# Batch 0's k over SyncE's queue with one add on VectorE, softmax in double steps, batch 1's attention placed late in tile 0

## The chip, the cores and the metric

One core of one Trainium2 chip. The metric is the device time of one execution in microseconds (us), lower is better. The profile's span (first to last instruction) is some 2 us shorter than that time. A run's state is "fast" or "slow"; only fast runs are compared. In the profiles PE is TensorE (PEld its weight loads), DVE is VectorE, ACT ScalarE, POOL GpSimd and SP SyncE.

## The reference

```python
# q, k, v: batch 8, heads 8, sequence 576, head size 64, float32
k_p = k.reshape(B, H, 72, 8, D).mean(axis=3)       # pooled over 8 rows
v_p = v.reshape(B, H, 72, 8, D).mean(axis=3)
scores = q @ k_p.T / sqrt(D)                       # softmax over 72
x = (softmax(scores) @ v_p)                        # to 4608 tokens x 512
h = x @ w_in                                       # 512 -> 2048
out = (h * cos(h)) @ w_out                         # 2048 -> 512
```

## The kernel before

The program order of each engine is as written. Tokens are worked in nine tiles of 512: an up-projection (64 matmuls of 512 columns), then a down-projection (64 more). A batch has 576 tokens, so tile t needs batches up to t (tile 8 up to 7); batch t+1's attention, for the next tile, is woven between the down matmuls of tile t. Batch 0's attention comes first, alone. The kernel uses PSUM as six banks in three pairs (`banks`) and two single ones (`obanks`). Cut and abridged:

```python
def step(b, i, pair):                    # one of 8 softmax steps of a batch: head pair i//2, half i%2
    cs, ao = pair[:, 0, :], pair[:, 1, :]
    sums(b, i, cs)                       # 2 matmuls with ones
    values(b, i, ao)                     # 2 matmuls with pooled v
    inverse(b, i, cs)                    # ScalarE: Ln, then Exp(-x)
    normal(b, i, ao)                     # VectorE: xT = ao * inverse
...
load_kv_cast(0, "k", k, 2)               # all of these on GpSimd's queue, fp32 cast to bf16
...
load_q(0, 2)
load_kv_cast(0, "v", v)
for cg in range(4): load_w_in(cg)
load_kv_cast(1, "k", k); load_q(1); load_kv_cast(1, "v", v)
for cg in range(4): load_w_out(cg)
...
    if t == 0:                           # batch 1: transposes and pooling ahead of the down-projection
        ...
        fill = [(i * 7 // 2, f) for i, f in enumerate(main)]
    else:                                # later batches
        early = [k_transpose, q_transpose, q_transpose_rem]        # written as lambdas
        main = att_main(b, [banks[1], banks[0]], banks[2])         # two score pairs, one pair for steps
        fill = [(4 + 4 * i, f) for i, f in enumerate(early)]
        fill += [(16 + (i * 5) // 2, f) for i, f in enumerate(main)]   # entry, before which down matmul
```

The softmax here doesn't subtract the row's maximum and nothing guards it: scores larger than these inputs give would overflow.

## Time and profile before

| | before |
|---|---|
| time, median of 4 runs | 361.46 us (360.49 to 362.04) |
| span of the profiled run | 358.6 us |
| batch 0's attention | 0 to 30.6 us |
| tile 0, up and down | 30.6 to 78.1 us |
| each of six tiles with attention | 36.80 us |
| each of two tiles without | 27.6 us |

The stages are read from the chain of waits, where the up-projections stand out as rows of 40 to 64 matmuls. "Starts effectively" below is the time at which an up-projection without a gap would have had to start to be where it is.

### The profile page before, as it was taken

What the parts mean: (1) busy time and instruction counts of PE and PEld (TensorE: products, weight loads), DVE (VectorE), ACT (ScalarE), POOL (GpSimd) and SP (SyncE); (2) the same over time, 40 slices, a digit from 0 to 9 for tenths busy, and PEclk for the clock granted to TensorE, in tenths of its full rate; (3) what the DMA queues carried; (4) which work ended last, traced back from release to release, by engine and by line L of the source; (5) the groups of instructions that cost most, each with busy time, mean ns of one, the idle gap of its engine ahead of it and who ended that gap; (6) DMA issues with size and microseconds to landing.
All of it is one profiled execution on the core that took longest, in us unless ns stands there. A gap on an engine that the chain in (4) does not pass through costs nothing.

```text
span 358.6 us, 4924 instructions
## 1 busy us (share of the span) xinstructions
PE 328.5 (92%) x1958; PEld 137.6 (38%) x1992; DVE 156.4 (44%) x201; ACT 191.8 (53%) x280; POOL 126.9 (35%) x84
## 2 busy tenths in 40 slices
PE   2787979989998999899989998999899999999995
PEld 2332532334423443344234432443244324444442
DVE  0222741136623672357235733573347434723731
ACT  1472634646575657655675666565656575602610
POOL 8533219800990089108910693059200000000000
PEclk9999987999999999999999999999999999999999
DMA  8999995179426951686087707680110001012011
GB/s 99 190 205 200 223 184 96 14 170 181 84 60 95 197 98 56 99 177 118 29 124 162 133 31 125 139 155 29 50 41 0 31 36 54 0 59 60 0 54 63
DMA packets 31494, 35.18 MB, mean 98 GB/s; under 512 B 5936, under 2 KB 20528, under 8 KB 31472
## 3 DMA queue, kind: packets, MB, share of 16 engines
q0 software_dynamic: 20224, 13.64, 27.0%
q1 hardware_dynamic: 11248, 21.24, 25.1%
q8 instruction: 15, 0.25, 0.3%
q14 instruction: 7, 0.06, 0.0%
HBM read 36.70 MB, written 9.44 MB: 129 GB/s over the span
## 4 chain that ended last, share of the span: by engine, by line
PE 88%; DVE 3%; ACT 3%; issue 2%; DMA 2%; POOL 1%; DVEq 0%; POOLq 0%
PE bank L258 35%; PE obank L266 34%; PE bank L199 4%; PE bank L208 4%; PE bank L222 3%; PE bank L168 2%; PE bank L150 2%; PE bank L266 2%; DVE xT L227 2%; DMA q_main<-in_q_dram 2%; ACT inv L214 1%; ACT lnc L212 1%; POOL k_b L87 1%; DVE o_sb L271 1%; DVE qT L171 1%
## 5 line engine op out<-in xcount | busy, mean ns | idle before, releaser
L266 PE MATMUL obank<-w_out_sb,g_sb 128*128 128x512 bf16 x522 | 138.0, 383 | 2.6 <-issue 2.1
L258 PE MATMUL bank<-xT,w_in_sb 128*128 128x512 bf16 x566 | 126.7, 382 | 0.8 <-issue 0.3
L262 ACT ACTIVATE cos<-bank,half_pi 128x1024 f32<-128x1024 f32 x72 | 80.2, 1114 | 75.7 <-PE bank L258 75.1
L263 DVE TENSOR_TENSOR g_sb<-bank,cos 128x1024 bf16<-128x1024 f32 x72 | 88.2, 1225 | 54.0 <-ACT cos L262 54.0
L117 POOL TENSOR_TENSOR kv_st<-kv_st 72x2048 f32<-72x2048 f32 x12 | 54.2, 4518 | 105.8 <-DMA kv_st<-in_k_dram 105.8
L258 PEld LDWEIGHTS <-w_in_sb 128*128 128x128 bf16 x576 | 56.5, 98 | 69.1 <-issue 2.4
L266 PEld LDWEIGHTS <-g_sb 128*128 128x128 bf16 x576 | 45.9, 98 | 60.0 <-issue 15.0
L227 DVE TENSOR_TENSOR xT<-bank,inv 128x288 bf16<-128x288 f32 x64 | 29.3, 458 | 88.9 <-ACT inv L214 84.7
L202 ACT ACTIVATE ex<-bank 72x576 bf16<-72x576 f32 x64 | 41.0, 641 | 36.7 <-PE bank L199 35.2
L212 ACT ACTIVATE lnc<-bank 128x288 f32<-128x288 f32 x56 | 23.0, 411 | 32.2 <-PE bank L222 32.2
L271 DVE COPY o_sb<-obank 128x512 f32<-128x512 f32 x34 | 23.4, 687 | 29.4 <-PE obank L266 29.4
L214 ACT ACTIVATE inv<-lnc 128x288 f32<-128x288 f32 x64 | 28.3, 443 | 2.0
L118 POOL TENSOR_TENSOR kv_st<-kv_st 72x1024 f32<-72x1024 f32 x12 | 28.2, 2349 | 0.9
L208 PE MATMUL bank<-ex,ones 72*64 72x288 bf16 x112 | 17.5, 307 | 6.3 <-DVE xT L227 6.3
L222 PE MATMUL bank<-ex,vp 72*64 72x288 bf16 x128 | 20.1, 303 | 3.1 <-DVE xT L227 3.1
L199 PE MATMUL bank<-qT,kpT 64*72 64x288 bf16 x128 | 21.5, 331 | 0.5 <-DVE qT L183 0.5
L208 PEld LDWEIGHTS <-ones 72*64 72x64 bf16 x128 | 8.5, 109 | 32.7 <-issue 32.7
L199 PEld LDWEIGHTS <-kpT 64*72 64x72 bf16 x128 | 7.4, 110 | 27.0 <-issue 27.0
L171 DVE COPY qT<-bank 128x2048 bf16<-128x2048 bf16 (+1 forms) x9 | 9.9, 1106 | 4.2 <-PE bank L168 4.2
L168 PE MATMUL bank<-identity,q_main 128*64 128x128 bf16 x256 | 9.7, 232 | 2.0 <-DMA q_main<-in_q_dram 1.2
L246 ACT ACT_TABLE_LOAD x8 | 10.3, 1283 | 0.9 <-PEq L389 0.7
L249 ACT ACT_TABLE_LOAD x8 | 10.3, 1283 | 0.1
(36 smaller groups left out, 109.0 us busy)
## 6 DMA issues: line engine op xcount, KB each, us to landing
out_dram<-o_sb SPq DMA_DIRECT2D x32, 256.0 KB, 2.3
kv_st<-in_k_dram SPq DMA_DIRECT2D x5, 1024.0 KB, 8.6
kv_st<-in_v_dram SPq DMA_DIRECT2D x5, 1024.0 KB
q_main<-in_q_dram POOLq DMA_DIRECT2D x7, 512.0 KB, 6.1
w_in_sb<-in_moe_w_in_dram POOLq DMA_DIRECT2D x4, 512.0 KB, 12.1
w_out_sb<-in_moe_w_out_dram POOLq DMA_DIRECT2D x4, 512.0 KB, 13.7
v_b<-in_v_dram POOLq DMA_DIRECT2D x2, 512.0 KB, 12.0
kv_st<-in_k_dram POOLq DMA_DIRECT2D x1, 1024.0 KB, 18.7
```

Source lines behind the costliest of these rows:

```text
L117: eng.tensor_tensor(out=s[:, :, 0:4, :], in0=s[:, :, 0:4, :], in1=s[:, :, 4:8, :], op=ADD)
L118: eng.tensor_tensor(out=s[:, :, 0:2, :], in0=s[:, :, 0:2, :], in1=s[:, :, 2:4, :], op=ADD)
L199: nc.tensor.matmul(pair[:Sp, hp, :SEG], lhsT=kpT[hp * 64:hp * 64 + 64, pj, :], rhs=qT[hp * 64:hp * 64 + 64, pj, sg * SEG:(sg + 1) * SEG])
L202: nc.scalar.activation(out=ex, in_=pair[:Sp, :, :SEG], func=ACTF.Exp, scale=scale / POOL)
L208: nc.tensor.matmul(cs[hp * 64:hp * 64 + 64, :SEG], lhsT=ones[:Sp, :], rhs=ex[:, hp, :])
L214: nc.scalar.activation(out=inv, in_=lnc, func=ACTF.Exp, scale=-1.0)
L222: nc.tensor.matmul(ao[hp * 64:hp * 64 + 64, :SEG], lhsT=vp[:, 2 * pj + hp, :], rhs=ex[:, hp, :])
L227: nc.vector.tensor_mul(out=xT[:, pj, c0:c0 + SEG], in0=ao[:, :SEG], in1=att.pop(("inv", b, i)))
L258: nc.tensor.matmul(h[:, j, :], lhsT=w_in_sb[fc // 4][:, ki, (fc % 4) * 128:(fc % 4 + 1) * 128], rhs=xT[:, ki, t * TILE:(t + 1) * TILE], st ...
L262: nc.scalar.activation(out=cos, in_=h, func=ACTF.Sin, bias=half_pi[:, :1])
L263: nc.vector.tensor_mul(out=g_sb[:, 2 * fp:2 * fp + 2, :], in0=h, in1=cos)
L266: nc.tensor.matmul(o, lhsT=g_sb[:, fc, ms * 128:(ms + 1) * 128], rhs=w_out_sb[fc // 4][:, fc % 4, :], start=(fc == 0), stop=(fc == FFCH - 1))
```

## The change

Its intent: get the first q earlier by moving k off GpSimd's queue; have fewer, longer softmax instructions; and let tile 0's down-projection run before batch 1's data are needed, with the output weights loaded earlier for it. The core of the diff, abridged (lambdas and other lines are left out):

```diff
+    def load_k_halves(b):                       # fp32, no cast, SyncE's queue
+        for j in range(2):
+            st = kvst.tile([Sp, H, POOL, D], FP32, ...)[:, 0:hs]
+            ... nc.sync.dma_start(out=o, in_=i.rearrange("h p n -> p h n"))
+    def pool_k_half(b, j, bank):
+        nc.vector.tensor_tensor(out=kb, in0=st[:, :, 0:4, :], in1=st[:, :, 4:8, :], op=ADD)
+        pool_k_mm(b, bank, kb, range(2 * j, 2 * j + 2))      # 4 rows left instead of 8
...
+    def sums(b, j, sg, cs):                     # two head pairs: 4 matmuls, Ln and Exp of 2 x 288
+    def values(b, j, sg, ao):                   # 4 matmuls; normal() multiplies 2 x 288 at once
+    def att_main(b):
+        sc, cs, ao = banks[0], banks[1], banks[2]            # one score pair
...
-    load_kv_cast(0, "k", k, 2)
+    load_k_halves(0)
+    load_q(0, 2)
...
+    for cg in range(4):
+        load_w_out(cg)                          # ahead of batch 1's k, q, v
...
+            if t == 0:
+                early = [pool_k_mm(1), q_transpose(1), q_transpose_rem(1), pool_v_mm(1)]
+                at, first, gap = [36, 44, 46, 50], 48, 1
+            else:
+                at, first, gap = [2, 6, 10], 14, 3
+            fill = list(zip(at, early))
+            fill += [(first + gap * i, f) for i, f in enumerate(att_main(b))]
```

Batch 0's order on PE also changes: the first scores come before the second half of k and q, and v is pooled before all values.

More of the change, by code (lines that the diff above doesn't have):

```diff
@@ L40 @@
     SEG = S // 2
-    NSTEP = 2 * KCH
     EX = 6
@@ L48 @@
     wpool = ctx.enter_context(tc.tile_pool(name="wpool", bufs=1))
-    kvb = ctx.enter_context(tc.tile_pool(name="kvb", bufs=4))
+    kvb = ctx.enter_context(tc.tile_pool(name="kvb", bufs=3))
     kvst = ctx.enter_context(tc.tile_pool(name="kvst", bufs=2))
@@ L79, in load_kv, with load_kv_cast @@
         staged[which, b] = st
-    def load_kv_cast(b, which, src, halves=1):
+    def load_kv_cast(b, which, src):
         st = kvb.tile([Sp, H, POOL, D], BF16, name=f"{which}_b", tag="kv_b")
-        hs = H // halves
-        for j in range(halves):
-            for o, i in by_rows(st[:, j * hs:(j + 1) * hs].rearrange("p h t d -> p h (t d)"),
-                                kv_view(src, b)[j * hs:(j + 1) * hs]):
-                nc.gpsimd.dma_start(out=o, in_=i.rearrange("h p n -> p h n"))
-        staged[which, b] = st
+        for o, i in by_rows(st.rearrange("p h t d -> p h (t d)"), kv_view(src, b)):
+            nc.gpsimd.dma_start(out=o, in_=i.rearrange("h p n -> p h n"))
+        staged[which, b] = st
+    def load_k_halves(b):
+        hs = H // 2
+        for j in range(2):
+            st = kvst.tile([Sp, H, POOL, D], FP32, name="kv_st", tag="kv_st")[:, 0:hs]
+            for o, i in by_rows(st.rearrange("p h t d -> p h (t d)"), kv_view(k, b)[j * hs:(j + 1) * hs]):
+                nc.sync.dma_start(out=o, in_=i.rearrange("h p n -> p h n"))
+            staged["k", b, j] = st
     def load_q(b, halves=1):
@@ L131, in heads, with pool_k_mm @@
         return x[:, 2 * pj:2 * pj + 2]
-    def pool_k_mm(b, bank, pjs):
-        kb = staged["k", b]
+    def pool_k_mm(b, bank, kb, pjs):
         if ("kpT", b) not in att:
             att["kpT", b] = asb.tile([128, KCH, Sp], BF16, name="kpT", tag="kpT")
-        ps = bank[:, 0:KCH * Sp].rearrange("p (j n) -> p j n", j=KCH)
-        for pj in pjs:
-            for t in range(POOL):
+        n, rows = len(pjs), kb.shape[2]
+        ps = bank[:, 0:n * Sp].rearrange("p (j n) -> p j n", j=n)
+        for i in range(n):
+            for t in range(rows):
                 for hp in range(2):
-                    nc.tensor.matmul(ps[hp * 64:hp * 64 + 64, pj, :], lhsT=kb[:, 2 * pj + hp, t, :],
-                                     rhs=identity[:Sp, :Sp], start=(t == 0), stop=(t == POOL - 1))
-        sl = slice(pjs[0], pjs[-1] + 1)
-        nc.vector.tensor_copy(out=att["kpT", b][:, sl, :], in_=ps[:, sl, :])
+                    nc.tensor.matmul(ps[hp * 64:hp * 64 + 64, i, :], lhsT=kb[:, 2 * i + hp, t, :],
+                                     rhs=identity[:Sp, :Sp], start=(t == 0), stop=(t == rows - 1))
+        nc.vector.tensor_copy(out=att["kpT", b][:, pjs[0]:pjs[-1] + 1, :], in_=ps)
+    def pool_k_half(b, j, bank):
+        st = staged.pop(("k", b, j))
+        kb = asb.tile([Sp, H // 2, POOL // 2, D], BF16, name="k_sum", tag="k_sum")
+        nc.vector.tensor_tensor(out=kb, in0=st[:, :, 0:4, :], in1=st[:, :, 4:8, :], op=ADD)
+        pool_k_mm(b, bank, kb, range(2 * j, 2 * j + 2))
     def pool_v_mm(b, bank):
@@ L162, in q_transpose @@
         n = len(pjs)
-        ps = bank.rearrange("p a n -> p (a n)").bitcast(BF16)[:, 0:n * 512].rearrange(
+        if len(bank.shape) == 3:
+            bank = bank.rearrange("p a n -> p (a n)")
+        ps = bank.bitcast(BF16)[:, 0:n * 512].rearrange(
             "p (j t n) -> p j t n", t=4, j=n)
@@ L193, in k_transpose, with scores @@
         att["kpT", b] = kpT
-    def scores(b, i, pair):
-        pj, sg = i // 2, i % 2
+    def scores(b, pj, sg, pair):
         kpT, qT = att["kpT", b], att["qT", b]
@@ L202, in scores @@
         nc.scalar.activation(out=ex, in_=pair[:Sp, :, :SEG], func=ACTF.Exp, scale=scale / POOL)
-        att["ex", b, i] = ex
-    def sums(b, i, cs):
-        ex = att["ex", b, i]
-        for hp in range(2):
-            nc.tensor.matmul(cs[hp * 64:hp * 64 + 64, :SEG], lhsT=ones[:Sp, :], rhs=ex[:, hp, :])
-    def inverse(b, i, cs):
-        lnc = asb.tile([128, SEG], FP32, name="lnc", tag="lnc")
-        nc.scalar.activation(out=lnc, in_=cs[:, :SEG], func=ACTF.Ln)
-        inv = asb.tile([128, SEG], FP32, name="inv", tag="inv", bufs=EX)
+        att["ex", b, pj, sg] = ex
@@ L214, in inverse @@
+    def sums(b, j, sg, cs):
+        for i in range(2):
+            ex = att["ex", b, 2 * j + i, sg]
+            for hp in range(2):
+                nc.tensor.matmul(cs[hp * 64:hp * 64 + 64, i, :SEG], lhsT=ones[:Sp, :], rhs=ex[:, hp, :])
+        lnc = asb.tile([128, 2, SEG], FP32, name="lnc", tag="lnc", bufs=1)
+        nc.scalar.activation(out=lnc, in_=cs[:, :, :SEG], func=ACTF.Ln)
+        inv = asb.tile([128, 2, SEG], FP32, name="inv", tag="inv")
         nc.scalar.activation(out=inv, in_=lnc, func=ACTF.Exp, scale=-1.0)
-        att["inv", b, i] = inv
@@ L217, in values @@
-    def values(b, i, ao):
-        ex = att.pop(("ex", b, i))
+        att["inv", b, j, sg] = inv
+    def values(b, j, sg, ao):
         vp = pooled["v", b]
-        pj = i // 2
-        for hp in range(2):
-            nc.tensor.matmul(ao[hp * 64:hp * 64 + 64, :SEG], lhsT=vp[:, 2 * pj + hp, :], rhs=ex[:, hp, :])
-    def normal(b, i, ao):
-        pj, sg = i // 2, i % 2
-        c0 = b * S + sg * SEG
-        nc.vector.tensor_mul(out=xT[:, pj, c0:c0 + SEG], in0=ao[:, :SEG], in1=att.pop(("inv", b, i)))
@@ L229, in step @@
-    def step(b, i, pair):
-        cs, ao = pair[:, 0, :], pair[:, 1, :]
-        sums(b, i, cs)
-        values(b, i, ao)
-        inverse(b, i, cs)
-        normal(b, i, ao)
-    def att_main(b, score_pairs, value_pair):
-        n = len(score_pairs)
-        main = [lambda: scores(b, 0, score_pairs[0])]
-        for i in range(NSTEP):
-            if i + 1 < NSTEP:
-                main.append(lambda i=i: scores(b, i + 1, score_pairs[(i + 1) % n]))
-            main.append(lambda i=i: step(b, i, value_pair))
+        for i in range(2):
+            pj = 2 * j + i
+            ex = att.pop(("ex", b, pj, sg))
+            for hp in range(2):
+                nc.tensor.matmul(ao[i][hp * 64:hp * 64 + 64, :SEG], lhsT=vp[:, 2 * pj + hp, :], rhs=ex[:, hp, :])
@@ new lines, in normal, with score, value, f @@
+    def normal(b, j, sg, ao):
+        c0 = b * S + sg * SEG
+        inv = att.pop(("inv", b, j, sg))
+        if isinstance(ao, list):
+            for i in range(2):
+                nc.vector.tensor_mul(out=xT[:, 2 * j + i, c0:c0 + SEG], in0=ao[i][:, :SEG], in1=inv[:, i, :])
+        else:
+            nc.vector.tensor_mul(out=xT[:, 2 * j:2 * j + 2, c0:c0 + SEG], in0=ao[:, :, :SEG], in1=inv)
+    def att_main(b):
+        todo = [(j, sg) for sg in range(2) for j in range(2)]
+        sc, cs, ao = banks[0], banks[1], banks[2]
+        def score(n, i):
+            j, sg = todo[n]
+            return lambda: scores(b, 2 * j + i, sg, sc)
+        def value(n):
+            j, sg = todo[n]
+            def f():
+                values(b, j, sg, [ao[:, 0, :], ao[:, 1, :]])
+                normal(b, j, sg, ao)
+            return f
+        main = [score(0, 0), score(0, 1)]
+        for n, (j, sg) in enumerate(todo):
+            if n + 1 < len(todo):
+                main.append(score(n + 1, 0))
+            main.append(lambda j=j, sg=sg: sums(b, j, sg, cs))
+            if n + 1 < len(todo):
+                main.append(score(n + 1, 1))
+            main.append(value(n))
@@ L289 @@
     nc.gpsimd.memset(half_pi, math.pi / 2.0)
-    load_q(0, 2)
     load_kv_cast(0, "v", v)
@@ L297 @@
     load_kv_cast(1, "v", v)
-    for cg in range(4):
-        load_w_out(cg)
     load_kv(2, "k", k, nc.gpsimd)
@@ L303 @@
     exp_tables()
-    LAG = 4
-    for j in range(2):
-        pjs = range(2 * j, 2 * j + 2)
-        pool_k_mm(0, obanks[j], pjs)
-    for j in range(2):
-        pjs = range(2 * j, 2 * j + 2)
-        q_transpose(0, banks[2 * j], pjs)
-        q_transpose_rem(0, banks[1][:, 0, :], pjs)
-    for i in range(2):
-        scores(0, i, banks[i])
-    for i in range(NSTEP + LAG):
-        if i < NSTEP:
-            sums(0, i, obanks[i % 2])
-            inverse(0, i, obanks[i % 2])
-            if i + 2 < NSTEP:
-                scores(0, i + 2, banks[i % 2])
-        if i == LAG - 1:
-            pool_v_mm(0, banks[2][:, 0, :])
-        if i >= LAG:
-            values(0, i - LAG, banks[2][:, 0, :])
-            normal(0, i - LAG, banks[2][:, 0, :])
+    pool_k_half(0, 0, obanks[0])
+    q_transpose(0, banks[2], range(0, 2))
+    q_transpose_rem(0, banks[2][:, 1, :], range(0, 2))
+    scores(0, 0, 0, banks[0])
+    scores(0, 1, 0, banks[1])
+    pool_k_half(0, 1, obanks[1])
+    q_transpose(0, obanks[0], range(2, 4))
+    q_transpose_rem(0, obanks[1], range(2, 4))
+    sums(0, 0, 0, banks[2])
+    scores(0, 0, 1, banks[0])
+    scores(0, 1, 1, banks[1])
+    pool_v_mm(0, obanks[1])
+    todo = [(0, 0), (0, 1), (1, 0), (1, 1)]
+    for n, (j, sg) in enumerate(todo):
+        values(0, j, sg, obanks)
+        normal(0, j, sg, obanks)
+        if n + 1 < 4:
+            sums(0, *todo[n + 1], banks[2])
+        if n + 2 < 4:
+            for i in range(2):
+                scores(0, 2 * todo[n + 2][0] + i, todo[n + 2][1], banks[i])
     sin_tables()
@@ L330 @@
             up(t, fp)
-            if t == 0 and fp == 5:
-                pool_k_mm(1, obanks[0], range(KCH))
         more = b < B
+        mms = [(ms, fc) for ms in range(4) for fc in range(FFCH)]
         fill = []
-        if t == 0:
-            outs = [obanks[0], obanks[1], banks[2][:, 0, :], banks[2][:, 1, :]]
-            mms = [(ms, fc) for cg in range(4) for ms in range(4) for fc in range(4 * cg, 4 * cg + 4)]
-            exp_tables()
-            q_transpose(1, banks[0])
-            q_transpose_rem(1, banks[1][:, 0, :])
-            pool_v_mm(1, banks[1][:, 1, :])
-            main = att_main(1, [banks[0]], banks[1])
-            fill = [(i * 7 // 2, f) for i, f in enumerate(main)]
-        else:
-            outs = [obanks[ms % 2] for ms in range(4)]
-            mms = [(ms, fc) for ms in range(4) for fc in range(FFCH)]
-            if more:
+        if more:
+            if t == 0:
+                early = [lambda: pool_k_mm(b, banks[0][:, 0, :], staged["k", b], range(KCH)),
+                         lambda: q_transpose(b, banks[1]),
+                         lambda: q_transpose_rem(b, banks[0][:, 1, :]),
+                         lambda: pool_v_mm(b, banks[2][:, 0, :])]
+                at, first, gap = [36, 44, 46, 50], 48, 1
+            else:
                 early = [lambda: k_transpose(b, banks[2][:, 0, :]),
@@ L350 @@
                          lambda: q_transpose_rem(b, banks[2][:, 1, :])]
-                main = att_main(b, [banks[1], banks[0]], banks[2])
-                fill = [(4 + 4 * i, f) for i, f in enumerate(early)]
-                fill += [(16 + (i * 5) // 2, f) for i, f in enumerate(main)]
-                exp_tables()
-        if more and t > 0 and b + 1 < B:
-            load_kv(b + 1, "k", k)
-            load_kv(b + 1, "v", v)
-            load_q(b + 1)
+                at, first, gap = [2, 6, 10], 14, 3
+            fill = list(zip(at, early))
+            fill += [(first + gap * i, f) for i, f in enumerate(att_main(b))]
+            fill.sort(key=lambda x: x[0])
+            exp_tables()
+            if t > 0 and b + 1 < B:
+                load_kv(b + 1, "k", k)
+                load_kv(b + 1, "v", v)
+                load_q(b + 1)
         fi = 0
@@ L363 @@
                 fi += 1
-            down_mm(outs[ms], ms, fc)
+            down_mm(obanks[ms % 2], ms, fc)
             if fc == FFCH - 1:
-                down_out(t, ms, outs[ms])
+                down_out(t, ms, obanks[ms % 2])
         while fi < len(fill):
```

## The prediction

> **What bounds the kernel now.** I first read the page's chain that ended last, by engine, then cut the span into stages: batch 0's attention, token tile 0 (up-projection, then down-projection with batch 1's attention between its matmuls), six equal tiles that each carry one more batch's attention, and two tiles without attention.
>
> The chain by engine:
>
> ```profile
> PE 88%; DVE 3%; ACT 3%; issue 2%; DMA 2%; POOL 1%; DVEq 0%; POOLq 0%
> ```
>
> Stretches of the span (start:end, length; busy time of PE, PEld, DVE, ACT, POOL with instructions in brackets; granted clock, DMA's busy share, GB/s):
>
> ```profile
> 0.00:31.00 31.00, 18.01 (x157) 9.01 (x159) 6.39 (x15) 13.18 (x26) 17.48 (x32) 1.00 1.16 169
> 31.00:49.80 18.80, 17.46 (x158) 8.59 (x159) 10.34 (x11) 10.11 (x9) 4.20 (x6) 1.00 1.24 206
> 49.80:78.28 28.48, 25.36 (x122) 8.95 (x125) 7.51 (x15) 13.37 (x26) 17.79 (x8) 0.88 0.63 98
> 78.28:115.08 36.80, 35.45 (x214) 14.38 (x216) 17.72 (x23) 22.88 (x34) 17.79 (x8) 1.00 0.60 116
> ...
> 299.08:326.70 27.62, 27.51 (x127) 12.54 (x128) 12.56 (x12) 8.91 (x8) 0.00 (x0) 1.00 0.10 39
> ```
>
> The tile without attention takes 27.62 us for 128 matmuls of 512 columns: 0.216 us each, PE without a gap. No change to waits can shorten that. A tile with attention takes 36.80, so its attention costs 9.2 us of PE's time; there are six. The share of DMA, over 1, says that it is saturated through the first two stretches and TensorE's clock granted at 0.88 in the third. The gains can lie in attention's 9.2 us per tile and in the first 78 us.
>
> PE's own waits (total, times, longest):
>
> ```profile
> PE obank L142 <- DMA k_b<-in_k_dram: 6.9, 2, 5.5
> PE bank L208 <- DVE xT L227: 6.3, 7, 0.9
> PE bank L222 <- DVE xT L227: 3.1, 6, 0.6
> ...
> PE bank L150 <- DVE qT L183: 1.1, 1, 1.1
> ```
>
> The second line is the steady loss: once per tile, 0.9 us. The timeline of a steady tile shows where: the last softmax step follows the one before it after only two down matmuls, and both use one PSUM pair, so PE waits for the normalisation:
>
> ```profile
> 111.65 0.46 DVE L227 TENSOR_TENSOR xT<-bank,inv 128x288 bf16<-128x288 f32 x1 [0.85 <-ACT inv L214]
> ...
> 112.16 0.31 PE L208 MATMUL bank<-ex,ones 72*64 72x288 bf16 x2 [0.93 <-DVE xT L227]
> ```
>
> The third line of waits is batch 0's tail, where one bank serves all values: the seven last normalisations follow each other at 1.07 us. Its timeline also shows:
>
> ```profile
> 10.13 1.07 PE L168 MATMUL bank<-identity,q_main 128*64 128x128 bf16 x16 [0.90 <-DMA q_main<-in_q_dram]
> ...
> 13.32 0.65 ACT L202 ACTIVATE ex<-bank 72x576 bf16<-72x576 f32 x1 [11.30 <-PE bank L199]
> ...
> 18.30 3.63 PE L150 MATMUL bank<-v_b,identity 72*72 72x512 bf16 x8
> ```
>
> **What the Trainium skill says.** "TensorE: Matmul & The Clock Gate", part 1: 512 columns take 426.7 ns while the array is cold, 215.7 ns once it has been busy some 3.4 us. The trace agrees: 0.216 above, but weight loads 0.425 apart in v's pooling (18.7 to 20.9) and in the first up matmuls (31.4 to 33.9). "ScalarE: Activation LUTs", What ACT_TABLE_LOAD costs: 186 ns plus 0.833 ns per element with immediate operands. 288 elements give 426 (trace: 411 for Ln, 443 for the inverse), 576 give 666 (trace: 641 for the softmax Exp). So doubling an activation saves one fixed part. "VectorE: DVE Perf Modes": two-source fp32 runs at one element per cycle of 0.96 GHz; 1024 of them are 1067 ns before overhead; the trace's 1024-element product, one source in PSUM, takes 1225. "DMA: Bandwidth & Descriptors", Issuing engines are not separate DMA queues: another issuing engine saves only issue time. The trace shows what that is on GpSimd: 0.57 to 0.79 us per issue, with four k issues ahead of q's first.
>
> **The change, part by part.**
>
> *Batch 0.* k goes as fp32 over SyncE, so q is issued from about 1.2 us instead of 4.4. Both share the bandwidth, so I put k's first half at about 5, q's at 7 (q was used at 10.1), second halves by 9. Added: per k half a VectorE add of 72x1024, about 1.1 us; removed: half of the pooling matmuls (32 took 1.17, 16 take 0.6). Scores now precede the second half: q transposes 7.0 to 8.1, copies to 9.0, first Exp about 9.4 instead of 13.3. But that isn't the gain, because v stands in PE's order before the values: v was issued at 7.1 and landed 7.6 later, near 15. The same 3.5 MB of fp32 come ahead of its end, started half a microsecond earlier, so I take 14.2. Pooling cold 3.6, copy 0.7: values begin at about 18.9. The chain from there, by the durations above (Ln 0.65, inverse 0.68, Exp 0.64, cold matmul groups 0.4 to 0.5): second sums 0.45 later, Ln, inverse and two Exps end at +3.55, third sums, Ln, inverse, two Exps at +6.8, fourth sums, Ln, inverse at +8.7, two products of 0.46 at +9.7. The first up group needs the last of these for its fourth chunk, so the up-projection effectively starts at +8.5 = 27.4. Before: 30.6. **Gain 3.2.**
>
> *Tile 0.* Up from 27.4: 64 x 0.216 = 13.8, plus 1.7 for eight cold ones; batch 1's k pooling (1.2) has left it: ends 42.9 (before 47.4). Down: 36 matmuls 7.8, k pooling 1.3, 8 matmuls 1.7, q transposes 1.2, and 1.7 until both copies to qT are done (they end after PE has passed the remainder and four matmuls, so 0.4 of it is idle): first score at 56.6. From there entries come after every single down matmul, and ScalarE is nearly the bound: 8 Exps of 0.64, 4 Ln and 4 inverses make 10.4 us, while the one score pair lets PE run only one Exp ahead. Walking the 16 entries in order, with 1.9 for v's warm pooling, I get PE waits of about 0.5 at four scores and the last sums, and 0.85 in the next up-projection for the last product: 14.8 us. Tile 1 starts at 71.4, before 78.1: **gain 6.7 in all, 3.5 beyond batch 0.** What pays is what the third stretch lost: PE idle 0.73, 0.64 and 1.1 around batch 1's q and v, and the cold clock after it.
>
> *Output weights first.* They land about 8 us earlier, k, q and v of batch 1 some 8 us later (v at about 43 instead of 35). Both are ahead of use (42.9 for weights, 52 for k, past 56 for v). Worth nothing by itself; it is what the later placing of batch 1 permits.
>
> *Six steady tiles.* PE's work is unchanged: one score group and one step cost together 1.905 (start to start of scores) less five down matmuls 1.08 = 0.83; eight make 6.6, k and q transposes 1.6, the wait 0.93, together 9.1 of the 9.2. After: still 8 score pairs, 8 sum pairs, 8 value pairs in 16 entries, now 3 matmuls apart, the last two too. The last sums have their Exp ready about 0.6 early and the last values find their bank free; 0.93 goes. New: scores use one pair only. A score reaches its Exp in 0.35 and frees the bank 0.64 later, 1.0 in all; the next score comes 0.24 + 3 x 0.216 + 0.1 = 1.0 later, so the first three scores of a tile may wait 0.05 to 0.1. Net 0.83 x 6 = **5.0**. Fewer, longer VectorE and ScalarE instructions save busy time that PE doesn't wait for. The last two tiles don't change.
>
> Sum: 6.7 + 5.0 = 11.7; 361.6 - 11.7 = about 350.
>
> **Rivals.**
> - *The single score pair becomes the bound in steady tiles.* The 1.0 against 1.0 above speaks for it at the tile's start; against it, later scores are two entries apart (2 us). A wait of 0.8 per tile would undo the 5.0: 355.
> - *Tile 0's packed softmax runs by ScalarE's latency, or the array goes cold again.* 16 entries within 16 matmuls; if each of 8 scores waits 0.5 more, +4; half clock over 5 us costs 2.5. Against: PE still has some 80% to do in that stretch. 353 to 354.
> - *v lands no earlier, or later, because k's queue takes turns with GpSimd's.* Each microsecond goes straight to the end: 351 to 352. If it lands at 13, PE isn't at the pooling before about 13.5 and the gain is up to 0.7 more: 349.
> - *All of batch 0's head start reaches the end* (first Exp 4 us earlier): 349. Against: v, above.
>
> **Range and chances.** The steady part is safest (0.93 seen in every tile), tile 0 the least safe, and it errs both ways by 3 us. Two per cent is 354.4, which needs two rivals at once. Predicted 350, range 346 to 354.
>
> **What would show it.** Steady tiles of about 35.95 without a wait for xT at the sums; short waits at the first scores for Exp. First Exp near 9.4; v's pooling at 14 to 15, in cold steps of 0.425; first up matmul near 27.5; tile 1 from about 71.4, clock 1.00 in tile 0's down-projection. Wrong if steady tiles stay at 36.5 or more, or tile 1 starts after 75.

## The result and the profile after

| | before | after |
|---|---|---|
| time, median of 4 runs | 361.46 us | 351.08 us (350.99 to 351.85) |
| ratio | | 0.972 (95% interval 0.9695 to 0.9746) |
| span | 358.6 us | 349.2 us |

A ratio is the mean time of one kernel's fast runs over that of the other's in the same rounds, so it is not quite the ratio of the medians. All outputs are right.

In the chain that ended last, PE's share is as it was:

```profile
PE 88%; ACT 4%; DMA 4%; DVE 1%; POOL 1%; issue 1%; ACTq 0%; POOLq 0%
```

The stretches of the kernel after (columns as in the prediction): batch 0, tile 0's up-projection, its down-projection with batch 1, two steady tiles, a tile without attention.

```profile
0.00:31.10 31.10, 15.53 (x126) 7.40 (x127) 7.95 (x15) 10.71 (x17) 14.48 (x27) 1.00 1.26 175
31.10:46.40 15.30, 14.74 (x63) 6.29 (x62) 8.54 (x9) 9.37 (x9) 4.76 (x8) 1.00 1.39 197
46.40:74.65 28.25, 25.89 (x223) 11.64 (x222) 9.43 (x13) 13.11 (x19) 17.82 (x8) 1.00 0.71 130
74.65:110.54 35.89, 35.62 (x215) 14.27 (x215) 17.19 (x20) 21.91 (x27) 17.77 (x8) 1.00 0.75 128
110.54:146.43 35.89, 35.89 (x218) 14.39 (x216) 17.07 (x19) 21.64 (x27) 17.80 (x8) 1.00 0.60 113
303.79:331.42 27.63, 27.63 (x130) 12.54 (x128) 12.57 (x13) 8.90 (x8) 0.00 (x0) 1.00 0.12 39
```

The steady tile is 0.91 shorter and PE has no gap in it: in the fifth row its busy time is the stretch. The first row ends half a microsecond later than batch 0's stage did before. Its clock of 1.00 is no measurement: the trace's clock records begin with the first change (at 34.2 here, 33.8 before), and the view counts the time before as full clock. PE's own waits in the whole kernel after (total, times, longest):

```profile
PE obank L146 <- DVE k_sum L153: 11.4, 2, 8.5
PE bank L221 <- ACT ex L214: 1.8, 3, 0.8
PE bank L211 <- ACT ex L214: 1.3, 3, 0.5
PE bank L284 <- DVE xT L243: 0.9, 1, 0.9
...
PE obank L159 <- DMA v_b<-in_v_dram: 0.8, 1, 0.8
```

The sums (L221) no longer wait for xT anywhere. Of the three waits of sums for Exp two are in batch 0; the three of scores (L211) and the one of the up-projection (L284) are tile 0's. None is in a steady tile. Batch 0's timeline:

```profile
7.22 1.22 DVE L153 TENSOR_TENSOR k_sum<-kv_st 72x1024 bf16<-72x1024 f32 x1 [7.22 <-DMA kv_st<-in_k_dram]
...
11.38 1.18 ACT L214 ACTIVATE ex<-bank 72x576 bf16<-72x576 f32 x2 [9.36 <-PE bank L211]
...
13.24 1.22 DVE L153 TENSOR_TENSOR k_sum<-kv_st 72x1024 bf16<-72x1024 f32 x1 [1.89 <-DMA kv_st<-in_k_dram]
...
14.52 0.69 PE L146 MATMUL obank<-identity,k_sum 72*64 72x72 bf16 x16 [2.94 <-DVE k_sum L153]
...
18.31 3.60 PE L159 MATMUL obank<-v_b,identity 72*72 72x512 bf16 x8 [0.79 <-DMA v_b<-in_v_dram]
```

The first Exp came 1.9 earlier than before (13.3), but then PE waited 2.94 for k's second half, which landed only at 13.2. That put it at v's pooling at 17.5, and there it waited 0.79 more for v, which landed at 18.2 (near 15.3 before). So the head start was lost at k's second half, and the last 0.8 of it at v.

| stage | before, us | after, us | gain | predicted |
|---|---|---|---|---|
| up-projection of tile 0 starts effectively | 30.6 | 31.1 | -0.5 | 3.2 |
| tile 1 starts effectively | 78.28 | 74.65 | 4.1 more | 3.5 more |
| six steady tiles | 6 x 36.80 | 6 x 35.89 | 5.5 | 5.0 |
| sum | | | 9.1 | 11.7 |

Both times of tile 1 are boundaries of the stretches; the 78.1 above and in the prediction is the record of the first matmul itself, 0.16 earlier. The span fell by 9.4; the small rest is in the tail and in the boundaries read to a tenth. By medians the time fell by 10.4.

### The profile page after: what moved, and what is told of

The parts are those of the page before. It is cut to its first block, busy times and chain, and to the rows that moved or that the text cites. A ratio compares the mean times of both kernels' runs of the same rounds, so it can differ in the third digit from the quotient of the medians.

```text
span 349.2 us, 4752 instructions
## 1 busy us (share of the span) xinstructions
PE 326.5 (93%) x1960; PEld 136.4 (39%) x1960; DVE 154.3 (44%) x175; ACT 181.6 (52%) x216; POOL 124.4 (36%) x80
## 4 chain that ended last, share of the span: by engine, by line
PE 88%; ACT 4%; DMA 4%; DVE 1%; POOL 1%; issue 1%; ACTq 0%; POOLq 0%
PE obank L292 38%; PE bank L284 36%; PE bank L211 4%; DMA v_b<-in_v_dram 4%; PE bank L221 3%; PE bank L234 3%; PE bank L179 2%; ACT inv L225 1%; ACT lnc L223 1%; ACT ex L214 1%; PE obank L159 1%; PE bank L159 0%; POOL q_main L100 0%; PE bank L191 0%; DVE qT L182 0%
## 5 line engine op out<-in xcount | busy, mean ns | idle before, releaser
L292 PE MATMUL obank<-w_out_sb,g_sb 128*128 128x512 bf16 x576 | 148.6, 381 | 0.0
L284 PE MATMUL bank<-xT,w_in_sb 128*128 128x512 bf16 x576 | 127.6, 382 | 1.4 <-DVE xT L243 0.9
L284 PEld LDWEIGHTS <-w_in_sb 128*128 128x128 bf16 x576 | 56.6, 98 | 71.0 <-issue 4.3
L243 DVE TENSOR_TENSOR xT<-bank,inv 128x576 bf16<-128x576 f32 x28 | 21.2, 758 | 67.7 <-PE bank L234 49.3
L297 DVE COPY o_sb<-obank 128x512 f32<-128x512 f32 x36 | 24.9, 691 | 41.5 <-PE obank L292 41.0
L223 ACT ACTIVATE lnc<-bank 128x576 f32<-128x576 f32 x32 | 20.8, 650 | 28.2 <-PE bank L221 27.9
L225 ACT ACTIVATE inv<-lnc 128x576 f32<-128x576 f32 x32 | 21.9, 683 | 1.0
L211 PE MATMUL bank<-qT,kpT 64*72 64x288 bf16 x128 | 20.4, 323 | 1.5 <-ACT ex L214 1.3
L211 PEld LDWEIGHTS <-kpT 64*72 64x72 bf16 x128 | 8.0, 111 | 25.1 <-issue 25.1
L221 PE MATMUL bank<-ex,ones 72*64 72x288 bf16 x128 | 15.6, 315 | 2.0 <-ACT ex L214 1.8
L234 PE MATMUL bank<-ex,vp 72*64 72x288 bf16 x112 | 12.2, 298 | 0.0
L146 PE MATMUL obank<-identity,k_sum 72*64 72x72 bf16 x32 | 1.4, 256 | 11.4 <-DVE k_sum L153 11.4
L221 PEld LDWEIGHTS <-ones 72*64 72x64 bf16 x128 | 5.5, 113 | 14.8 <-issue 14.5
```

The lines of the kernel that those rows point to most:

```text
L211: nc.tensor.matmul(pair[:Sp, hp, :SEG], lhsT=kpT[hp * 64:hp * 64 + 64, pj, :], rhs=qT[hp * 64:hp * 64 + 64, pj, sg * SEG:(sg + 1) * SEG])
L221: nc.tensor.matmul(cs[hp * 64:hp * 64 + 64, i, :SEG], lhsT=ones[:Sp, :], rhs=ex[:, hp, :])
L223: nc.scalar.activation(out=lnc, in_=cs[:, :, :SEG], func=ACTF.Ln)
L225: nc.scalar.activation(out=inv, in_=lnc, func=ACTF.Exp, scale=-1.0)
L284: nc.tensor.matmul(h[:, j, :], lhsT=w_in_sb[fc // 4][:, ki, (fc % 4) * 128:(fc % 4 + 1) * 128], rhs=xT[:, ki, t * TILE:(t + 1) * TILE], st ...
L292: nc.tensor.matmul(o, lhsT=g_sb[:, fc, ms * 128:(ms + 1) * 128], rhs=w_out_sb[fc // 4][:, fc % 4, :], start=(fc == 0), stop=(fc == FFCH - 1))
```

## The experiments

All ran against the kernel before on the same chip in each group of four: its median was 361.19 in the first group (e1, e9, e8, e4), 361.11 in the second (e2, e3, e6, e7; seven of its eight runs are those of the first), 360.99 in the third (the rest, on another chip). The changed kernel was not run again with them; it stands at 351.08, ratio 0.972. Every ratio below is to the kernel before.

| run | median, us | ratio (95% interval) |
|---|---|---|
| e1_k_cast | 349.32 | 0.9671 (0.9649 to 0.9692) |
| e9_k_fp32_gpsimd | 350.93 | 0.9715 (0.9701 to 0.973) |
| e8_hold_w_in | 350.27 | 0.9706 (0.9685 to 0.9728) |
| e4_wout_late | 351.87 | 0.9785 (0.9717 to 0.9854), unclear |
| e2_single_steps | 357.15 | 0.9892 (0.9876 to 0.9909) |
| e3_before_spread | 354.55 | 0.982 (0.9805 to 0.9835) |
| e6_tile0_spread | 349.59 | 0.9678 (0.9664 to 0.9693) |
| e7_all | 346.76 | 0.9596 (0.9574 to 0.9619) |
| e5_v_later | 350.89 | 0.9706 (0.9678 to 0.9734) |
| e10_warm | 342.10 | 0.947 (0.9446 to 0.9494) |
| e11_single_spread | 346.51 | 0.9585 (0.9557 to 0.9614) |
| e12_warm_single | 342.00 | 0.947 (0.9442 to 0.9498) |

### Why v came late: k's bytes, the second queue, or the weights

**e1_k_cast**: k back on GpSimd's queue with the cast, pooled over eight rows (abridged: k's tile becomes bf16, and its pool has four buffers again).

```diff
-                nc.sync.dma_start(out=o, in_=i.rearrange("h p n -> p h n"))    # fp32 staging tile
+                nc.gpsimd.dma_start(out=o, in_=i.rearrange("h p n -> p h n"))  # bf16 tile
...
-        nc.vector.tensor_tensor(out=kb, in0=st[:, :, 0:4, :], in1=st[:, :, 4:8, :], op=ADD)
-        pool_k_mm(b, bank, kb, range(2 * j, 2 * j + 2))
+        pool_k_mm(b, bank, st, range(2 * j, 2 * j + 2))
```

> Changed kernel, but batch 0's k goes back to GpSimd's queue with the cast to bf16 and eight-row pooling. In the changed kernel v landed at 18.2 us instead of the predicted 14.2 and the up-projection began effectively at 31.1, no earlier than before (30.6). Theory W (bytes written): fp32 k writes twice the bytes in SBUF, and the DMA engines are bound by some 206 GB/s written, so 0.59 MB more cost about 2.9 us; with the cast v lands near 15 and the up-projection starts at about 29: time 2 to 2.5 us below the changed kernel (348.7 to 349). Theory Q (queues take turns): also v near 15, same time. Rival N: the order of PE's work and ScalarE set the start, not v: within 0.7 us of the changed kernel.

Measured 349.32, 1.8 below the changed kernel's median. From its timeline, v's pooling and the matmuls of the up-projection after its last wait for batch 0's xT:

```profile
15.66 3.60 PE L159 MATMUL obank<-v_b,identity 72*72 72x512 bf16 x8
...
29.28 2.29 PE L284 MATMUL bank<-xT,w_in_sb 128*128 128x512 bf16 x5 [0.56 <-DVE xT L241]
```

The pooling started 2.65 earlier and waited for nothing; the up-projection's third matmul came at 29.28 instead of 31.94, the same 2.65. Theories W and Q both hold so far; N falls. But tile 1 started only 1.5 earlier. The weight loads show why: in this run they stood 0.425 apart (half clock; 0.216 is full) until 33.9, in the changed kernel's until 34.3. The array became fast at nearly the same time in both, so part of the earlier start went into more slow matmuls.

**e9_k_fp32_gpsimd**: the same fp32 k and the same add, but issued on GpSimd's queue ahead of q.

```diff
-                nc.sync.dma_start(out=o, in_=i.rearrange("h p n -> p h n"))
+                nc.gpsimd.dma_start(out=o, in_=i.rearrange("h p n -> p h n"))
```

> Changed kernel, but k's fp32 halves are issued on GpSimd's queue, ahead of q, with VectorE's add kept: one queue, the same bytes written. Theory W: v lands at 18 or later (q is issued 2.5 us later), time equal to the changed kernel or up to 1 us above it. Theory Q: with one queue in order k, q, v nothing takes turns: v lands near 15 to 15.5, time 1.5 to 2.5 us below the changed kernel.

Measured 350.93, as the changed kernel. The view of v's tile gives the time from issue to landing of v's two loads (shortest, median, longest), first in the changed kernel, then here:

```profile
DMA to landing us min/median/max: 12.4/12.6/12.7
```

```profile
DMA to landing us min/median/max: 8.2/8.3/8.4
```

v's last load was issued at about 5.5 in the changed kernel and at about 7.9 here, so v landed at 18.2 and at about 16.2. With the cast (e1) it landed at about 15.6. So of the 2.6 between the changed kernel and e1 about 2 belong to the second queue, and about 0.6 to the added bytes. W as I had stated it (v at 18 or later) fell; Q was nearer, with W as a part. The time hardly moved, because here q is issued 2.5 later, the first Exp ran at 13.3 instead of 11.4, and PE reached v's pooling only at 17.4: v no longer gated.

**e8_hold_w_in**: nothing of the input weights is issued before v has landed.

```diff
     load_kv_cast(0, "v", v)
+    probe = consts.tile([Sp, 8], BF16, name="probe")
+    nc.gpsimd.tensor_copy(out=probe, in_=staged["v", 0][:, 7, 7, 0:8])
     for cg in range(4):
         load_w_in(cg)
```

> Changed kernel, but GpSimd reads eight elements per row of v before it issues the input weights, so nothing of them is in flight ahead of v's end (0.3 MB written of q0's queue beyond q and v had moved by then). Theory W: 0.3 MB at 206 GB/s is 1.5 us at most, v lands at 17 to 17.5; the weights then land up to 3 us later and may stall the first up-projection: time between -1 and +3 us of the changed kernel. Rival O (v is late because the weights overtake it): v lands at 15, up-projection starts at 28 if weights allow.

v landed 0.6 earlier (12.0 instead of 12.7 after its issue at 5.5), near the 17 to 17.5 expected of W. Rival O, which had v at 15, falls: the weights hold v up by 0.6 at most. The up-projection went on 0.64 earlier after its last wait (31.30), but the array became fast only at 36.4, and the time, 350.27, is within the noise of the changed kernel's.

Why two queues are slower than one for the same bytes I did not settle. The trace's packets say that 512-byte packets of q took longer beside k's 2 KB ones (97 ns on average in the first 20 us, 68 in the kernel before). But k's own packets had ended at 12.0 in the changed kernel, 6 us before v landed, so taking turns with k can't be all of it. In e8, where nothing followed v, DMA's busy share fell from 1.42 (14 to 14.5 us) to 0.24 (16 to 16.5), v's last packet ended at 16.4 and v was released at 17.5: some of the 16 engines seem to have been done long before the others, and v waits for the last. What makes them uneven stays open.

**e4_wout_late**: output weights again behind batch 1's loads.

```diff
-    for cg in range(4):
-        load_w_out(cg)
     load_kv_cast(1, "k", k)
     load_q(1)
     load_kv_cast(1, "v", v)
+    for cg in range(4):
+        load_w_out(cg)
```

> Changed kernel with the output weights again behind batch 1's k, q, v. My step: worth nothing by itself. Weights land at about 44 us against their first use at 46.4: within 0.4 us of the changed kernel. Rival: they land after 46.4, the first down-projection waits: +1 to +3 us.

Three runs gave 350.93, 351.72 and 352.01; the fourth, 356.62, was marked slow, and the verdict is unclear. The profile decides: tile 1's up-projection goes on at 74.87 instead of 74.92 after its wait for xT, and the list of waits has none for a weight. Worth nothing, as predicted.

### What pays in the steady tiles

**e2_single_steps**: the changed kernel with the old softmax in the six steady tiles (abridged: the definitions of the old steps are left out).

```diff
-                at, first, gap = [2, 6, 10], 14, 3
+                at, first, gap = [4, 8, 12], 16, 2.5
-            fill += [(first + gap * i, f) for i, f in enumerate(att_main(b))]
+            main = att_main(b) if t == 0 else att_main1(b, [banks[1], banks[0]], banks[2])   # old steps
+            fill += [(first + int(gap * i), f) for i, f in enumerate(main)]
```

> Changed kernel, but the six steady tiles carry the softmax of before: single steps, score pairs alternating, the last two steps two down matmuls apart. My step: the changed steady tile took 35.89 us, before 36.80; with this undone the tile is 36.80 again with PE's wait of 0.93 for xT at the sums: 5.5 us above the changed kernel (356.6). Rival: the wait belonged to the placing of tile 0 or of loads, then the tile stays near 35.9.

Measured 357.15: 6.1 above the changed kernel. The wait is back, once in each of the six tiles (L274 is the old sums, L293 the old product), and the tile takes 36.80 again:

```profile
PE bank L274 <- DVE xT L293: 5.6, 6, 0.9
```

**e3_before_spread**: the kernel *before*, with one number changed.

```diff
-                fill += [(16 + (i * 5) // 2, f) for i, f in enumerate(main)]
+                fill += [(16 + (i * 5) // 2, f) for i, f in enumerate(main[:-1])] + [(58, main[-1])]
```

> The kernel before with one number changed: the last softmax step of a steady tile comes seven down matmuls after the one before it instead of two. Theory P (placing): what pays in steady tiles is that distance, not the doubling: tile 35.9, PE waits for xT at the sums only once (in tile 0): 5.4 us below before (355.8). Rival D (doubling): the double steps save PE or ScalarE something the tile needs, so this gains under 2 us. Rival E: the later last step delays the next tile's first up-projection by its normalisation: gain 2 to 4.

Measured 354.55, that is 6.6 below before, where 5.4 had been expected. Here are its steady tile in the view by stretches and its wait of sums for xT, which is left in tile 0 alone:

```profile
150.00:185.80 35.80, 35.80 (x218) 14.29 (x216) 17.73 (x24) 22.87 (x35) 17.77 (x8) 1.00 0.60 112
```

```profile
PE bank L208 <- DVE xT L227: 0.7, 1, 0.7
```

The tile is 35.80, no longer than with double steps (35.89). VectorE and ScalarE are as busy as before (17.73 and 22.87), and PE has no gap. Theory P holds, D and E fall: the distance between the last two steps alone gives the whole gain of the steady tiles. Whether double steps at the old distance would have given it too was not run. This one number is worth more than half of the change.

### Tile 0

**e6_tile0_spread**: batch 1's attention begins earlier and is spread.

```diff
-                at, first, gap = [36, 44, 46, 50], 48, 1
+                at, first, gap = [18, 26, 28, 31], 30, 2
```

> Changed kernel, but in tile 0's down-projection batch 1's k pooling starts at matmul 18 instead of 36 and the softmax entries come every second matmul from the 30th instead of every one from the 48th. The changed kernel's PE waits there: 1.3 (scores for Exp), 0.2 (sums for Exp), 0.2 (qT), 0.9 (next up-projection for xT): 2.6 in all. If the packing costs that, 2 to 2.3 us below the changed kernel (about 349). Rival: batch 1's v has not landed when its pooling comes at matmul 31 (about 55 us), then no gain or a loss.

Measured 349.59, 1.5 below the changed kernel. The waits it was to remove are gone but for 0.2 and 0.2:

```profile
PE bank L211 <- DVE qT L194: 0.2, 1, 0.2
PE bank L211 <- ACT ex L214: 0.2, 1, 0.2
```

Tile 0 from the end of its up-projection (47.9) to tile 1's effective start (73.3) took 25.4, against 28.1 in the changed kernel (46.57 to 74.65): 2.7 saved. In the profiled run 1.2 of it was given back in the up-projection, which took 15.82 for 62 matmuls instead of 14.63, with more of them slow. The edit is no reason for that: up to there the two programs are the same, and the array became fast at 36.7 here, at 34.3 there. The packing of batch 1 was thus right in keeping PE fed, but denser than need be.

**e5_v_later**: v of batch 0 pooled after the second sums (abridged).

```diff
-    pool_v_mm(0, obanks[1])
     todo = [(0, 0), (0, 1), (1, 0), (1, 1)]
+    sums(0, *todo[1], banks[2])
+    for i in range(2):
+        scores(0, 2 * todo[2][0] + i, todo[2][1], banks[i])
+    pool_v_mm(0, obanks[1])
     for n, (j, sg) in enumerate(todo):
         values(0, j, sg, obanks)
         normal(0, j, sg, obanks)
-        if n + 1 < 4: ...
+        if n + 2 < 4: ...                       # sums and scores one further ahead
```

> Changed kernel with one thing changed: batch 0's v is pooled after the second sums and third scores instead of ahead of them. In the changed kernel ScalarE stood idle 4.6 us while v was awaited, pooled and copied. If v's place in PE's order sets the start of the up-projection, the ScalarE work now lies beside the pooling and the up-projection starts 0.5 to 1 us earlier: 350.1 to 350.6. If the pooling's own 3.6 us at half clock sets it, wherever it stands: within 0.4 us.

Measured 350.89: no difference that these runs can show. The pooling now started at 20.1 and took 3.63 again; the up-projection started effectively at 30.3, 0.8 earlier than the changed kernel's 31.1, as the first theory had it. But the array became fast at 35.4, a microsecond later than there, and the weight loads of the down-projection began at 46.4 against 46.2. So whether v's place is worth anything these runs can't say; the 3.6 us of pooling at half clock are paid in either place.

### A version that beats both

**e7_all**: e1, e5 and e6 together (their edits as above).

> A version meant to beat both: k cast on GpSimd's queue, tile 0's softmax spread as in e6, and batch 0's v pooled after the second sums and third scores. Sum of parts: k cast -1.8 as measured, spread -2.2, v later -0.5: 346.5 to 347.5. If the start of the up-projection only moves into the cold clock (it warmed at 33.9 us in k cast's trace though the matmuls began at 27.7), 0.5 to 1 us of it is lost.

Measured 346.76, inside the expected range. Its up-projection starts at 28.9.

**e10_warm**: e7 with matmuls of zeros where PE would wait in batch 0.

```diff
+    zeros = consts.tile([128, 512], BF16, name="zeros")
+    nc.vector.memset(zeros, 0.0)
+    def warm(bank, n):
+        for _ in range(n):
+            nc.tensor.matmul(bank, lhsT=zeros[:, 0:128], rhs=zeros)
+    warm(banks[0][:, 0, :], 18)
     pool_k_half(0, 0, obanks[0])
+    warm(banks[0][:, 0, :], 4)                  # and 3, 5 and 3 more at later waits
```

> e7 with 33 extra matmuls of zeros (512 columns) where PE waits in batch 0: 18 before the first k, 4 before q, 3 before q's remainder, 5 before the second sums, 3 before the first values. They compute nothing; they keep the array busy. In e7 every matmul before about 34 us ran at half clock. If the clock is what the start still loses: v's pooling takes 1.8 instead of 3.6, weight loads of the first up matmuls stand 0.216 apart, 2.5 to 4 us below e7 (343 to 344.5). If zeros or gaps don't hold the clock up: the 33 cost 0.5 to 2 us, time above e7.

Measured 342.10, 4.7 below e7, more than the 2.5 to 4 expected. v's pooling in e7, then here:

```profile
18.69 3.63 PE L159 MATMUL obank<-v_b,identity 72*72 72x512 bf16 x8
```

```profile
16.56 1.92 PE L159 MATMUL obank<-v_b,identity 72*72 72x512 bf16 x8
```

The up-projection started at 24.3 instead of 28.9. So half clock had cost 4.6 us of batch 0. It isn't all won: the weight loads of the first up matmuls, from 24.7 to 27.3, stand 0.425 apart again, and the trace's clock record is 0.50 from 24.0 to 27.4.

**e11_single_spread**: e7 with the old single steps, the last of them at down matmul 58 (as in e3).

> e7 with the softmax of before in steady tiles (single steps), the last one seven down matmuls after the one before. Theory P (placing alone pays): steady tile 35.8 as in e3 against 35.89 with double steps: 0.5 us below e7 or equal (346.2 to 346.8). Theory D (doubling has a worth of its own): above e7 by 1 us or more.

Measured 346.51, equal to e7. Its steady tiles take 35.80. Placing alone pays here too.

**e12_warm_single**: e10 and e11 together.

> e10 and e11 together. If both are as expected, 343 to 344; parts add up because they lie in different stages.

Measured 342.00, equal to e10, just below the range expected. e10 and e12 are the fastest kernels: ratio 0.947 to the kernel before.

## Why the prediction was right, and where its steps were not

The time (350 predicted, 351.08 measured) was right, and so was the sum's larger part; batch 0's term was wrong.

- **Steady tiles**: right in mechanism and size (35.95 predicted, 35.89 measured, PE's wait of 0.93 gone). The short waits that I had allowed at a tile's first scores did not occur. What I did not see is that the double steps aren't needed for it and add nothing to it (e3, e11).
- **Tile 0**: the gain beyond batch 0 was 4.1 against 3.5. The down-projection took 28.25 (28.5 predicted), with the waits about where they were put: scores for Exp 1.3 in three places (four of 0.5 predicted), the up-projection for xT 0.9 (0.85). The clock stayed up in it: 1.00, where before it was 0.88. e6 confirms the size of the waits.
- **Output weights**: worth nothing, as stated (e4).
- **Batch 0**: the step that failed, at the arrival of k's second half and of v. It read: "second halves by 9", and "The same 3.5 MB of fp32 come ahead of its end, started half a microsecond earlier, so I take 14.2." k's second half landed at 13.2 and v at 18.2, and the gain was -0.5 instead of 3.2. With v at 14.2 as I had it, k's second half would still have kept PE from v's pooling until 17.5. The bytes *read* were the same, but k's fp32 halves write twice the bytes (about 0.6 us at v), and with a second queue v came about 2 us later (e9 against the changed kernel). I also put k's first half at 5, and it landed at 7.2, with q's at about 8.5 instead of 7 (7.2 after its issue at 1.26); the add took 1.22 instead of 1.1. The chain behind the values was right: 8.4 from the first values (22.69) to the effective start, 8.5 predicted. The sum ahead of it was not: 14.2, 3.6 and 0.7 make 18.5 and not 18.9. The third rival named this outcome, "v lands no earlier, or later, because k's queue takes turns with GpSimd's", with 351 to 352. Outcome and time are what happened; its reason is not shown, since k's packets had ended 6 us before v landed.
- **Clock**: I charged 1.7 for eight cold matmuls of the up-projection as a constant. It isn't one: the array became fast at 33.9 before, 34.3 after, 33.9 in e1, 33.4 in e9, 36.4 in e8 and 36.7 in e6, at no fixed time after the matmuls had begun. That gives or takes over a microsecond from run to run, and ate part of what e1 and e6 won in their profiled runs. What I overlooked: within a trace the clock's changes lie whole multiples of 3.41 us apart (33.84, 50.91 and 57.73 in the kernel before; 6.94, 24.01 and 27.42 in e10), and where this grid lies differs from run to run. So part of such a gain or loss is chance.

So the total came within 1.1 us because 3.7 us too much for batch 0 met 1.1 us too little for the other stages, 0.3 in the tail and about 1 us between span and time: that is luck. A reader should trust the two later stages of this prediction, not its first.

## What to carry to other kernels

When a step waits for the step before it on the same buffer, first look at how far apart they are placed: one number here gave all that a rewrite into longer instructions gave in those tiles. Before moving a load to another queue, count the bytes that it will write, and ask what is queued behind it; the loads that come last (here k's second half and v) decide, not the one that the change helps. And a phase in which PE waits often is paid for twice, in waits and in a half-rate clock; cheap matmuls in those waits gave 4.7 us, more than the other edits of that stage (e1 1.8, e8 0.8, e5 0.2).

## What the Trainium skill lacked or had wrong

- "DMA: Bandwidth & Descriptors" (Issuing engines are not separate DMA queues) says that transfers of different issuing engines interleave and that a second issuing engine saves only issue time. It doesn't say that it can cost: with the same fp32 k ahead of v, v landed at 18.2 us with k on SyncE's queue and at about 16.2 with k on GpSimd's (e9), though the latter issued v some 2.4 us later. Nor does it give a rate for loads that cast; while DMA's busy share was 1.24 (31 to 49.8 us of the kernel before) they and the weights moved 206 GB/s as the profile counts bytes, and the fp32 halves of k cost about 0.6 us more than the cast ones.
- "TensorE: Matmul & The Clock Gate", part 1, has the change to full clock vary by half a microsecond from run to run, by where the first matmul falls in a free-running window of some 3.4 us. The window agrees with these traces (changes of the clock whole multiples of 3.41 apart). The half microsecond does not: from the first uninterrupted up matmul to the first fast ones it was 2.4 us in the changed kernel (31.9 to 34.3) and 4.6 in e6 (32.1 to 36.7), whose program is the same up to there; 4.6 in e1 and 5.1 in e8.
- The same page asks to keep TensorE busy, but doesn't say that matmuls of zeros in a kernel's own waits pay; e10 shows 4.7 us.
- No page says that the profile's clock reads 1.00 where no change has been recorded yet: it does so in all of batch 0, in which matmuls of 512 columns came 0.425 us apart.
